# The first four blocks of a gated linear attention and MLP kernel loaded as pairs of neighbouring tokens, with a new order of the opening and w_in in fp32

## The chip, the cores and the metric

The kernel runs on one core of a Trainium2 chip. The core's engines work side by side, each through its own list of instructions in order: TensorE (PE in the profile; its weight loads are PEld), VectorE (DVE), ScalarE (ACT), GpSimd (POOL) and SyncE (SP), which here only issues transfers. Transfers run on 16 DMA engines. The metric is the time of one execution in microseconds; the median of three runs before the change is 194.14 us (193.95 to 194.42).

## The reference

Four sequences of 768 tokens with eight heads of 48 go through a gated linear attention, and its output, as rows of 384 numbers, through an MLP of width 2,048 with a squared relu.

```python
# q, k, v, alpha: (4, 8, 768, 48) fp32, alpha between 0.8 and 1
for t in range(S):
    state = alpha[:, :, t, :, None] * state + einsum('bhd,bhe->bhde', k[:, :, t], v[:, :, t])
    y[:, :, t] = einsum('bhd,bhde->bhe', q[:, :, t], state)
x = y.transpose(0, 2, 1, 3).reshape(3072, 384)
h = x @ w_in                      # 384 x 2048
r = maximum(h, 0)
out = (s * (r * r) + b) @ w_out   # 2048 x 384
```

## The kernel before

The 3,072 tokens are cut into 24 blocks of 128 tokens, six to a sequence (`NBLK`, `NCH`). A block goes through these steps; n is its number.

- Loads: alpha, k, q and v, one transfer each on SP (`load`, `load_one`, lines 121 to 127). The heads lie apart in memory, so each token and head is a run of 48 fp32 numbers, 192 B, and a block is 786 KB. Eight blocks fit at once (`NLD`).
- `ln` (ACT): logarithm of alpha. `cum` (line 191): on PE a product with an upper triangle of ones sums the logarithms along the tokens, and for the first five blocks four small products give the sum over the whole block; ACT then takes the exponential of the negative and of the positive sum. `vcast` (POOL): v in bf16.
- `qk` (DVE): k times the first exponential, q times the second. `tr`: eight PE transposes and one DVE copy to `qkT`. `amat`: eight PE products for A, then two DVE products with a triangular mask.
- `yp` (line 259): y from A and v, and from the state of the block before; also the block's part of the next state (`pst`); ACT copies y out of PSUM. `st` (POOL mainly): the new state. `xt`: three PE transposes of y and an ACT copy give the MLP's input.
- The MLP: `mp` makes 512 columns' worth of products with w_in in one PSUM bank, `rl` (ACT) the relu, `sq` (DVE) the square; `mm2` multiplies by w_out in four quarters (`o`), and ACT or DVE takes the result out. Blocks 0 and 1 form one group of 256 tokens for `mp`; each other block is a group by itself.

w_in comes in quarters of 512 columns on POOL's queue (`load_w_in`, line 129), where the transfer itself turns fp32 into bf16. w_out comes in quarters on SP and is scaled and cast on chip (`cast_w_out`). The bias and the stores of the first 14 blocks wait until later.

The order of all work is written out by hand. A list (lines 498 to 509) holds the opening: each entry is a function and its arguments, and each engine takes its instructions in the order in which the list calls them. Later blocks get positions from a formula (lines 514 to 543): block n is centred at 8n, with its steps at fixed distances; entries are sorted by position. Transfers stand in SP's list in the order of their issue: blocks 0 to 3 first (lines 440 to 446), then, from `weights_out` (line 473), w_out and blocks 4 to 7. `busy` (line 174) puts filler matmuls of 512 columns on PE whose result nobody reads; the list has sixteen of them among the first blocks. Eight PSUM banks are shared; `first_banks` says which one each piece of the opening uses.

```python
at(p - e, y, n)                                    # p = 8 * n
at(p + (2.5, 3.5, 5.5, 7.5)[u], m, group_of[n][0], u)
at(p + (8.5, 9.5, 12.5, 14.5)[u], o, n, u)
```

## Time and profile before

| | |
|---|---|
| median of three runs | 194.14 us |
| the profiled execution: its time, its span | 193.98 us, 192.2 us |
| PE, ACT, DVE, POOL busy | 94%, 61%, 77%, 34% of the span |
| chain that ended last | PE 82%, ACT 3%, DVE 2% |
| w_in products (L359) on PE, w_out products (L397) | 71.2 us busy, 68.3 us busy |
| relu (L373, ACT), one | 596 ns |
| square (L380, DVE), one | 493 ns |
| a steady block, from one w_out quarter at 76.91 to the same at 83.95 | 7.04 us |

The span runs from the first to the last instruction; the time includes what lies around it. Busy shares are averages over all stages. The chain is followed back from the last instruction to what each step waited for; 82% on PE says that for most of the span PE's own list set the pace. PE's busy time counts matmuls from start to end, and these overlap, so the distance between starts is the measure of what one costs.

### The profile page before, as it was taken

To read this page: it belongs to the slowest core of one execution; us is meant where nothing else is said; L and a number is where in the kernel's file an instruction comes from. 1 tells how busy PE (TensorE), PEld (TensorE's weight loads), DVE (VectorE), ACT (ScalarE), POOL (GpSimd) and SP (SyncE) were. 2 spreads that over 40 slices of the span, in tenths; PEclk is the share of its full clock that TensorE was granted. 3 is DMA by queue.
4 is the path that set the end of the run, shared out by engine and by line. 5 is a ranking of instruction groups with operands and counts; after the bars stand their busy time and mean duration, and the time that the engine had idled before them with its cause. 6 is when DMAs were issued, how large, how long until landed. Compare 5 with 4: busy or idle time off the path is not lost.

```text
span 192.2 us, 5966 instructions
## 1 busy us (share of the span) xinstructions
PE 179.9 (94%) x2378; PEld 143.6 (75%) x2380; DVE 148.6 (77%) x288; ACT 117.4 (61%) x240; POOL 64.4 (34%) x100
## 2 busy tenths in 40 slices
PE   0898799999999999999999999999999999999993
PEld 0575589665877788878887887887887888788782
DVE  5377877568668877988878996698988999997641
ACT  3355378815866576676676667776666657554540
POOL 6147922011310542652311562462302383262000
PEclk9999999999999999999999999999999999999999
DMA  6999999979994685682979367569958768436212
GB/s 121 190 185 185 191 223 320 326 155 192 188 153 82 132 135 91 109 151 35 206 110 162 57 114 138 107 91 195 206 118 184 148 146 164 93 121 246 85 41 82
DMA packets 113453, 28.74 MB, mean 150 GB/s; under 512 B 106627, under 2 KB 113426, under 8 KB 113426
## 3 DMA queue, kind: packets, MB, share of 16 engines
q1 hardware_dynamic: 111822, 26.79, 73.5%
q0 software_dynamic: 1600, 1.57, 5.2%
q8 instruction: 18, 0.29, 0.7%
q14 instruction: 9, 0.07, 0.1%
q10 hardware_dynamic: 4, 0.00, 0.0%
HBM read 25.19 MB, written 4.74 MB: 156 GB/s over the span
## 4 chain that ended last, share of the span: by engine, by line
PE 82%; ACT 3%; DVE 2%; issue 1%; ACTq 0%
PE h_ps L359 30%; PE o_ps L397 28%; PE ct_ps L229 5%; PE a_ps L244 3%; PE h_ps L311 2%; PE y_ps L272 2%; PE a_ps L397 2%; PE ct_ps L195 2%; PE y_ps L263 1%; PE a_ps L420 1%; PE p_ps L283 1%; ACT r_sb L373 1%; PE o_ps L359 1%; ACT w_out_bf L151 1%; PE a_ps L359 1%
## 5 line engine op out<-in xcount | busy, mean ns | idle before, releaser
L373 ACT ACTIVATE r_sb<-h_ps 128x512 bf16<-128x512 f32 x90 | 53.6, 596 | 35.0 <-PE h_ps L359 33.2
L359 PEld LDWEIGHTS <-w_in_bf 128*128 128x128 bf16 x1104 | 67.8, 98 | 6.8 <-issue 0.9
L359 PE MATMUL h_ps<-xd_all,w_in_bf 128*128 128x128 bf16 (+1 forms) x1056 | 71.2, 220 | 0.3 <-ACT xd_all L317 0.2
L397 PE MATMUL o_ps<-w_out_bf,gt_all 128*128 128x384 bf16 x336 | 68.3, 326 | 0.1
L380 DVE TENSOR_TENSOR gt_all<-r_sb 128x512 bf16<-128x512 bf16 x96 | 45.9, 493 | 25.4 <-ACT r_sb L373 24.5
L338 POOL TENSOR_TENSOR sd_sb<-t_sb,blast 48x192 bf16<-48x192 f32 x40 | 20.3, 508 | 77.7 <-DVE t_sb L333 45.2
L397 PEld LDWEIGHTS <-gt_all 128*128 128x128 bf16 x368 | 32.6, 98 | 16.2
L189 POOL CAST v_bf<-v_sb 128x384 bf16<-128x384 f32 x24 | 17.1, 717 | 32.2 <-DMA v_sb<-in_v_dram 27.6
L342 POOL TENSOR_TENSOR sc_sb<-t_sb,blast 112x384 f32<-112x384 f32 x16 | 21.6, 1347 | 1.2
L317 ACT ACTIVATE xd_all<-h_ps 128x384 bf16<-128x384 bf16 x23 | 11.3, 491 | 15.3 <-PE h_ps L311 15.3
L234 DVE COPY qkT<-ct_ps 112x1024 bf16<-112x1024 bf16 x24 | 16.4, 684 | 3.9 <-PE ct_ps L229 3.1
L252 DVE TENSOR_TENSOR am_a<-a_ps,mask 128x512 bf16<-128x512 f32 x24 | 16.4, 683 | 3.4 <-PE a_ps L244 3.4
L223 DVE TENSOR_TENSOR kb_sb<-k_sb,bi_sb 128x384 bf16<-128x384 f32 x24 | 13.7, 573 | 3.9 <-ACT bi_sb L206 3.6
L252 DVE TENSOR_TENSOR am_b<-a_ps,mask 128x512 bf16<-128x512 f32 x24 | 16.3, 680 | 0.0
L224 DVE TENSOR_TENSOR qb_sb<-q_sb,b_sb 128x384 bf16<-128x384 f32 x24 | 15.7, 655 | 0.0
L186 ACT ACTIVATE la_sb<-al_sb 128x384 bf16<-128x384 f32 x24 | 12.4, 517 | 3.8 <-DMA al_sb<-in_alpha_dram 3.7
L290 ACT ACTIVATE y_bf<-y_ps 128x384 bf16<-128x384 f32 x24 | 11.7, 490 | 4.6 <-PE y_ps L272 4.4
L229 PEld LDWEIGHTS <-qb_sb 128*112 128x112 bf16 x96 | 8.7, 136 | 5.1 <-DVE qb_sb L224 3.7
L229 PE MATMUL ct_ps<-ident,qb_sb 128*112 128x128 bf16 x96 | 10.1, 230 | 1.1 <-DVE qb_sb L224 1.1
L206 ACT ACTIVATE bi_sb<-ct_ps 128x384 f32<-128x384 f32 x20 | 9.7, 486 | 1.6 <-PE ct_ps L195 1.0
L244 PE MATMUL a_ps<-qkT 48*128 48x128 bf16 x192 | 9.8, 222 | 0.8 <-DVE qkT L234 0.4
L207 ACT ACTIVATE b_sb<-ct_ps 128x384 f32<-128x384 f32 x20 | 9.9, 494 | 0.0
(75 smaller groups left out, 196.2 us busy)
## 6 DMA issues: line engine op xcount, KB each, us to landing
al_sb<-in_alpha_dram SPq DMA_DIRECT2D x24, 192.0 KB
k_sb<-in_k_dram SPq DMA_DIRECT2D x24, 192.0 KB
q_sb<-in_q_dram SPq DMA_DIRECT2D x24, 192.0 KB
v_sb<-in_v_dram SPq DMA_DIRECT2D x24, 192.0 KB
w_out_st<-in_moe_w_out_dram SPq DMA_DIRECT2D x4, 768.0 KB
out_dram<-w_in_st SPq DMA_DIRECT2D x14, 192.0 KB
out_dram<-out_sb SPq DMA_DIRECT2D x9, 192.0 KB
w_in_bf<-in_moe_w_in_dram POOLq DMA_DIRECT2D x4, 384.0 KB, 6.6
```

What stands on the lines that cost most here:

```text
L189: nc.gpsimd.tensor_copy(out=v_bf[n % 3], in_=v_sb[n % NLD])
L224: nc.vector.tensor_tensor(out=qb_sb[n % 2][:, :, 0:48], in0=q_sb[n % NLD], in1=b_sb[n % 3], op=ALU.mult)
L229: nc.tensor.transpose(out=t_ps[0:112, x, p, :], in_=t.rearrange("a h d -> a (h d)")[:, 128 * p : 128 * p + 112], identity=ident,)
L234: nc.vector.tensor_copy(out=qkT_sb[n % 2][0:112].rearrange("a x p t -> a (x p t)"), in_=t_ps[0:112].rearrange("a x p t -> a (x p t)"),)
L244: nc.tensor.matmul(out=a_ps[e][:, p, :], lhsT=qkT[r0 : r0 + 48, 1, p, :], rhs=qkT[r0 : r0 + 48, 0, p, :], start=True, stop=True,)
L252: nc.vector.tensor_tensor(out=am_sb[e][n % 2], in0=a_ps[e], in1=mask4, op=ALU.mult)
L338: nc.gpsimd.tensor_tensor(out=sd[r, :, d], in0=t1_sb[r, :, d], in1=bl[r].to_broadcast([48, NP, 48]), op=ALU.mult)
L342: nc.gpsimd.tensor_tensor(out=sc_sb[0:112], in0=t1_sb[0:112], in1=bl[0:112].to_broadcast([112, NP, 96]), op=ALU.mult)
L359: nc.tensor.matmul(out=hp[:, jj * N : (jj + 1) * N], lhsT=w_in_bf[:, kk, 128 * j : 128 * (j + 1)], rhs=xd_sb[g][:, kk, 0:N], start=(kk == ...
L373: nc.scalar.activation(out=rs, in_=h_of.pop((g, u)), func=AF.Relu)
L380: nc.vector.tensor_tensor(out=gt_sb[g][:, u * 512 : (u + 1) * 512], in0=rs, in1=rs, op=ALU.mult)
L397: nc.tensor.matmul(out=op[:, 0:d_model], lhsT=gt_sb[g][:, j * N + t * C : j * N + (t + 1) * C], rhs=w_out_bf[:, j, :], start=(j == 0), sto ...
```

## The change

Blocks 0 and 1, and blocks 2 and 3, are loaded as pairs: 256 tokens in 128 rows, two neighbouring tokens in each row, so that a run in memory is 96 numbers, 384 B. "Block" 2i then holds the even tokens of the pair and block 2i+1 the odd ones while sums, A and the products with k and q are made; after the transposes, the copies (`qk_copy`) put q and k back so that the first 128 tokens (b = 0) and the last 128 (b = 1) can be addressed. The sums of a pair are two accumulated products each, with block-triangular matrices `D_bf` and `Ds_bf`; A is made in four parts (key parity s, head parity e) of eight small products; y and the state update take even and odd keys one after the other, with 64 rows each. The output of a pair's block is stored in two parts, of its even and its odd rows.

w_in is loaded in fp32 by SP, in the order of quarters 1, 2, 0, 3 among the other loads, and cast on ACT and DVE in twelve pieces. The group of 256 tokens goes: every block has its own `mp`. The functions of the steps are split by engine, and a new written list of 330 entries orders them as far as position 60; `rooms` gives their PSUM banks. Three filler matmuls are left. All of SP's loads up to block 7 are issued before the list. From position 60 on, the formula places the same work as before.

```diff
-    GROUPS = [2] + [1] * (NBLK - 2)
     UNITS = 5
-    assert sum(GROUPS) == NBLK
     NLD = 8
-    NFIRST = 4
+    PAIRS = [0, 2]
+    pair_of = {p + i: p for p in PAIRS for i in range(2)}
...
+    D_bf = sb.tile([128, 128], BF16, name="D_bf")
+    Ds_bf = sb.tile([128, 128], BF16, name="Ds_bf")
+    ones_p = sb.tile([128, 2], BF16, name="ones_p")
+    mask_p = [sb.tile([128, NP, 2, 64], BF16, name=f"mask_p{i}") for i in range(2)]
...
+    qkT_all = sb.tile([128, 2, 2 * NP * 128], BF16, name="qkT")
+    qkT_sb = [qkT_all[:, i].rearrange("a (x p t) -> a x p t", x=2, p=NP) for i in range(2)]
+    qkT_p = qkT_all.rearrange("a u y -> a (u y)").rearrange("a (x p b s i) -> a x p b s i", x=2, p=NP, b=2, s=2)
...
+    def load_pair(n, name):
+        whole, t = {"al": (al_all, alpha), "k": (k_all, k), "q": (q_all, q), "v": (v_all, v)}[name]
+        b, c = n // NCH, n % NCH
+        nc.sync.dma_start(
+            out=whole[:, n % NLD : n % NLD + 2].rearrange("a u x -> a (u x)").rearrange("a (h x) -> a h x", h=H),
+            in_=t[b, :, c * C : (c + 2) * C, :].rearrange("h (r s) d -> r h (s d)", s=2),
+        )
...
     def load_w_in(i):
         cols = slice(i * d_ff // 4, (i + 1) * d_ff // 4)
-        nc.gpsimd.dma_start(
-            out=w_in_bf[:, :, cols], in_=moe_w_in[:, cols].rearrange("(t r) f -> r t f", t=KT)
-        )
+        nc.sync.dma_start(out=w_in_st[:, :, cols], in_=moe_w_in[:, cols].rearrange("(t r) f -> r t f", t=KT))
+
+    def cast_w_in(i, kk, act):
+        cols = slice(i * d_ff // 4, (i + 1) * d_ff // 4)
+        if act:
+            nc.scalar.activation(out=w_in_bf[:, kk, cols], in_=w_in_st[:, kk, cols], func=AF.Copy)
+        else:
+            nc.vector.tensor_copy(out=w_in_bf[:, kk, cols], in_=w_in_st[:, kk, cols])
...
-    def busy(n, bank=o_ps):
+    def busy(n, key):
         for i in range(n):
             nc.tensor.matmul(
-                out=bank,
-                lhsT=U_bf,
-                rhs=mask4.rearrange("a p t -> a (p t)"),
+                out=room(key),
+                lhsT=D_bf,
+                rhs=mask_p[0].rearrange("a p s t -> a (p s t)"),
...
+    def cum_pair(n):
+        for s, m in ((0, D_bf), (1, D_bf if n > pair_of[n] else Ds_bf)):
+            nc.tensor.matmul(
+                out=room(("c", n))[:, 0:384], lhsT=m, rhs=la_sb[s][:, :, 0:48], start=(s == 0), stop=(s == 1)
+            )
+
+    def tot_pair(n):
+        for p in range(NP):
+            for s in range(2):
+                nc.tensor.matmul(
+                    out=room(("t", n))[0:112, 400 + 2 * p : 402 + 2 * p],
+                    lhsT=la_sb[s].rearrange("a h d -> a (h d)")[:, 128 * p : 128 * p + 112],
+                    rhs=ones_p,
+                    start=(s == 0),
+                    stop=(s == 1),
+                )
+
...
+    def qk_copy(n):
+        if n in pair_of:
+            nc.vector.tensor_copy(
+                out=qkT_p[0:112, :, :, :, n - pair_of[n]].rearrange("a x p b i -> a (x p) b i"),
+                in_=t_ps[0:112].rearrange("a x p (b i) -> a (x p) b i", b=2),
+            )
+            return
...
+    def amat_pair(n, s, e):
+
+        bank = room(("A", n, s, e)).rearrange("a (p x) -> a p x", p=NP)
+        r = slice(64 * e, 64 * e + 48)
+        for p in range(NP):
+            for b in range(2):
+                cols = slice(64 * b, 64 * b + 64)
+                nc.tensor.matmul(
+                    out=bank[cols, p, :],
+                    lhsT=qkT_p[r, 1, p, b, s],
+                    rhs=qkT_p[r, 0, p, b].rearrange("a s i -> a (s i)"),
+                    start=True,
+                    stop=True,
+                )
+
+    def mask_pair(n, s, e):
+        nc.vector.tensor_tensor(
+            out=am_sb[e][s].rearrange("a p t -> a (p t)"),
+            in0=room(("A", n, s, e)),
+            in1=mask_p[s].rearrange("a p s t -> a (p s t)"),
+            op=ALU.mult,
+        )
+
+    def y_pair(n):
+        p0 = pair_of[n]
+        c = n % NCH
+        rows = slice(64 * (n - p0), 64 * (n - p0) + 64)
+        if c > 0:
+            for p in range(NP):
+                nc.tensor.matmul(
+                    out=y_ps[:, 96 * p : 96 * p + 96],
+                    lhsT=qkT_p[0:112, 0, p, n - p0].rearrange("a s i -> a (s i)"),
+                    rhs=sd_sb[(n - 1) % 2][0:112, p, :],
+                    start=(p == 0),
+                    stop=False,
+                    skip_group_check=True,
+                )
+        for h in range(H):
+            for s in range(2):
+                nc.tensor.matmul(
+                    out=y_ps[:, 48 * h : 48 * h + 48],
+                    lhsT=am_sb[h % 2][s][rows, h // 2, :],
+                    rhs=v_bf[(p0 + s) % 3][rows, h, :],
+                    start=(c == 0 and h == 0 and s == 0),
+                    stop=(h == H - 1 and s == 1),
+                    skip_group_check=True,
+                )
+
+    def pst_pair(n):
+        p0 = pair_of[n]
+        rows = slice(64 * (n - p0), 64 * (n - p0) + 64)
+        for p in range(NP):
+            for s in range(2):
+                nc.tensor.matmul(
+                    out=pst[:, p, :],
+                    lhsT=kb_sb[(p0 + s) % 3].rearrange("a h d -> a (h d)")[rows, 128 * p : 128 * p + 128],
+                    rhs=v_bf[(p0 + s) % 3][rows, 2 * p : 2 * p + 2, :],
+                    start=(s == 0),
+                    stop=(s == 1),
+                )
+
...
+    rooms = {
+        ("A", 0, 0, 0): a1, ("A", 0, 0, 1): h1, ("A", 0, 1, 0): a0, ("A", 0, 1, 1): a1, ("A", 2, 0, 0): ct,
+        ("A", 2, 0, 1): o, ("A", 2, 1, 0): a1, ("A", 2, 1, 1): h1, ("c", 0): ct, ("c", 1): a0, ("c", 2): h0,
...
+    def mp(n, u):
+        hp = room((n, u))
+        for jj in range(4):
+            j = 4 * u + jj
             for kk in range(KT):
                 nc.tensor.matmul(
-                    out=hp[:, jj * N : (jj + 1) * N],
+                    out=hp[:, jj * C : (jj + 1) * C],
                     lhsT=w_in_bf[:, kk, 128 * j : 128 * (j + 1)],
-                    rhs=xd_sb[g][:, kk, 0:N],
+                    rhs=xd_sb[n][:, kk],
...
     def store(n, o):
+        if n in pair_of:
+            rows = out[n * C : (n + 1) * C, :].rearrange("(i s) m -> s i m", s=2)
+            for s in range(2):
+                nc.sync.dma_start(out=rows[s], in_=o[64 * s : 64 * s + 64])
+            return
...
+    load_pair(0, "al")
+    load_pair(0, "k")
+    load_pair(0, "q")
+    load_pair(0, "v")
+    load_pair(2, "al")
+    load_pair(2, "q")
+    load_pair(2, "v")
+    load_pair(2, "k")
+    load_one(4, al_sb, alpha)
+    load_w_in(1)
+    load_w_in(2)
+    load_w_in(0)
+    load_one(4, k_sb, k)
+    load_one(4, q_sb, q)
+    load_one(4, v_sb, v)
+    load_one(5, al_sb, alpha)
+    load_w_in(3)
+    load_one(5, q_sb, q)
+    load_one(5, k_sb, k)
+    load_one(6, al_sb, alpha)
+    load_one(5, v_sb, v)
+    load_one(6, q_sb, q)
+    load_one(6, k_sb, k)
+    load_w_out(0, 4)
+    load_w_out(4, 8)
+    load_one(6, v_sb, v)
+    load_w_out(8, 12)
+    load_w_out(12, 16)
+    load_one(7, al_sb, alpha)
+    load_one(7, q_sb, q)
+    load_one(7, v_sb, v)
+    load_one(7, k_sb, k)
...
-            (ln, 0), (vcast, 0), (cum, 0), (qk, 0), (spread,), (busy, 2), (tr, 0), (ln, 1), (busy, 1), (vcast, 1), (amat, 0), (cum, 1),
-            (busy, 3), (yp, 0), (qk, 1), (st, 0), (busy, 1), (tr, 1), (ln, 2), (xt, 0), (vcast, 2), (load_w_in, 0), (load_w_in, 1), (cum, 2), (busy, 1), (amat, 1),
-            (busy, 3), (yp, 1), (qk, 2), (st, 1), (busy, 1), (tr, 2), (ln, 3), (xt, 1), (load_w_in, 2), (vcast, 3), (load_w_in, 3), (cum, 3), (busy, 1), (amat, 2),
...
+            (spread,), (ln, 0), (ln, 1), (busy, 1, ("c", 0)), (cum_pair, 0), (cum_act, 0), (cum_pair, 1), (cum_act, 1),
+            (pst_pe, 5), (kb_mul, 0), (qb_mul, 0), (vcast, 0), (qb_mul, 1), (tot_pair, 0), (busy, 1, ("T", 0)),
+            (tr, 0, 0), (tr, 0, 1), (kb_mul, 1), (qk_copy, 0), (vcast, 1), (busy, 1, ("T", 1)), (tr, 1, 0), (tr, 1, 1),
+            (qk_copy, 1), (pst_pair, 0), (tot_act, 0), (ln, 3), (ln, 2), (cum_pair, 2), (amat_pair, 0, 1, 1), (t1, 0),
+            (cum_act, 2), (amat_pair, 0, 0, 1), (mask_pair, 0, 1, 1), (sd, 0), (vcast, 2), (amat_pair, 0, 0, 0),
+            (qb_mul, 2), (mask_pair, 0, 0, 1), (amat_pair, 0, 1, 0), (cum_pair, 3), (tot_pair, 2), (tr, 2, 0),
+            (mask_pair, 0, 0, 0), (cum_act, 3), (mask_pair, 0, 1, 0), (y_pair, 0), (kb_mul, 2), (pst_pair, 1),
+            (qb_mul, 3), (y_act, 0), (tr, 2, 1), (y_pair, 1), (xt_pe, 0), (tot_act, 2), (ln, 4), (kb_mul, 3),
+            (qk_copy, 2), (vcast, 3), (y_act, 1), (cast_w_in, 1, 1, True), (xt_act, 0), (tr, 3, 0), (t1, 1), (tr, 3, 1),
+            (cum_pe, 4), (pst_pair, 2), (sd, 1), (xt_pe, 1), (qk_copy, 3), (amat_pair, 2, 0, 0), (xt_act, 1),
+            (cum_act, 4), (cast_w_in, 2, 2, True), (cast_w_in, 2, 0, True), (cast_w_in, 2, 1, True),
+            (cast_w_in, 1, 2, False), (cast_w_in, 1, 0, False), (amat_pair, 2, 1, 0), (mask_pair, 2, 0, 0), (t1, 2),
+            (mp, 0, 1), (rl, 0, 1), (amat_pair, 2, 0, 1), (amat_pair, 2, 1, 1), (pst_pair, 3), (mp, 1, 1), (sd, 2),
+            (mask_pair, 2, 1, 0), (mask_pair, 2, 0, 1), (mask_pair, 2, 1, 1), (rl, 1, 1), (mp, 1, 2),
+            (cast_w_in, 0, 1, False), (cast_w_in, 0, 2, False), (cast_w_in, 0, 0, True), (y_pair, 2), (mp, 0, 2),
+            (mp, 0, 0), (rl, 1, 2), (y_act, 2), (rl, 0, 2), (sq, 0, 1), (qb_mul, 4), (xt_pe, 2), (y_pair, 3), (tr, 4, 0),
+            (kb_mul, 4), (t1, 3), (sq, 0, 2), (rl, 0, 0), (vcast, 4), (tr, 4, 1), (mp, 1, 0), (xt_act, 2), (y_act, 3),
+            (ln, 5), (rl, 1, 0), (sd, 3), (xt_pe, 3), (pst_pe, 4), (mp, 2, 1), (qk_copy, 4), (xt_act, 3), (rl, 2, 1),
+            (amat, 4), (cum_pe, 5), (cum_act, 5), (mp, 3, 2), (sq, 1, 1), (sq, 1, 2), (mask, 4, 1), (mask, 4, 0),
+            (mp, 3, 0), (sq, 0, 0), (cast_w_in, 3, 1, False), (cast_w_in, 3, 2, False), (qb_mul, 5), (rl, 3, 2),
+            (cast_w_in, 3, 0, True), (t1, 5), (mp, 2, 2), (mp, 2, 0), (y_pe, 4), (rl, 3, 0), (mp, 1, 3), (rl, 2, 2),
+            (y_act, 4), (rl, 1, 3), (tr, 5, 0), (xt_pe, 4), (rl, 2, 0), (xt_act, 4), (ln, 6), (kb_mul, 5), (sq, 3, 2),
+            (tr, 5, 1), (t1, 4), (sq, 3, 0), (sq, 2, 2), (qk_copy, 5), (mp, 0, 3), (sq, 1, 0), (rl, 0, 3), (mp, 2, 3),
+            (mp, 4, 0), (cum_pe, 6), (sq, 2, 1), (amat, 5), (rl, 2, 3), (mp, 4, 2), (cum_act, 6), (mask, 5, 0),
+            (mp, 4, 1), (mask, 5, 1), (vcast, 5), (sd, 4), (rl, 4, 2), (rl, 4, 0), (sq, 2, 0), (kb_mul, 6), (mp, 4, 3),
+            (qb_mul, 6), (sq, 4, 0), (sq, 1, 3), (rl, 4, 1), (y_pe, 5), (rl, 4, 3), (cast_w_out, 0, 2, False),
+            (vcast, 6), (y_act, 5), (mp, 3, 1), (mp, 3, 3), (vcast, 7), (load, 8), (cast_w_out, 2, 4, True), (tr, 6, 0),
+            (tr, 6, 1), (xt_pe, 5), (o_pe, 0, 0), (o_pe, 1, 0), (xt_act, 5), (o_pe, 4, 0), (sd, 5), (rl, 3, 3),
...
+    def late(pos, *what):
+        for fn, *args in what:
+            if pos >= OPEN:
+                at(pos, fn, *args)
```

## The prediction

> **What bounds the kernel now.** I read the page's slices first, then the TensorE timeline, then the landings of the loads in the ACT and POOL timelines.
>
> ```profile
> span 192.2 us, 5966 instructions
> PE   0898799999999999999999999999999999999993
> PEclk9999999999999999999999999999999999999999
> DMA  6999999979994685682979367569958768436212
> GB/s 121 190 185 185 191 223 320 326 155 192 188 153 82 132 135 91 109 151 35 206 110 162 57 114 138 107 91 195 206 118 184 148 146 164 93 121 246 85 41 82
> DMA packets 113453, 28.74 MB, mean 150 GB/s; under 512 B 106627, under 2 KB 113426, under 8 KB 113426
> ```
>
> A slice is 4.8 us. PE is full from slice 5 on, so it bounds the kernel. In the first five slices the DMA engines are full and move only 185 to 191 GB/s: these are the loads of blocks 0 to 3, rows of 192 B. In slices 6 and 7 (w_out, rows of 1,536 B) the same engines move 320.
>
> ```profile
> 4.51 0.48 PE L195 MATMUL h_ps<-la_sb,U_bf 128*128 128x384 bf16 x1 [4.51 <-ACT la_sb L186]
> ...
> 9.98 1.44 PE L176 MATMUL o_ps<-mask,U_bf 128*128 128x512 bf16 x3
> ...
> 14.95 0.82 PE L176 MATMUL o_ps<-mask,U_bf 128*128 128x512 bf16 x3
> ...
> 22.44 0.82 PE L359 MATMUL h_ps<-xd_all,w_in_bf 128*128 128x256 bf16 x6
> ...
> 71.69 0.81 PE L397 MATMUL o_ps<-w_out_bf,gt_all 128*128 128x384 bf16 x4
> ```
>
> Columns: start, time taken, operation. The three filler matmuls (L176) take 1.44 us at 9.98 and 0.82 us at 14.95: up to about 14.6 us PE runs at half speed, though the slices show PEclk as 9. The first product with w_in (L359) starts at 22.44. At 71.69 stands the third of the four w_out products of block 6. Both kernels issue the same work from there on, in one order, so 192.2 - 71.7 = 120.5 us are common, and the change lives in front of this point, which I call the cut.
>
> ```profile
> 3.93 0.52 ACT L186 ACTIVATE la_sb<-al_sb 128x384 bf16<-128x384 f32 x1 [1.92 <-DMA al_sb<-in_alpha_dram]
> ```
>
> ```profile
> 7.05 0.50 POOL L189 CAST v_bf<-v_sb 128x384 bf16<-128x384 f32 x1 [3.17 <-DMA v_sb<-in_v_dram]
> 11.26 0.84 POOL L189 CAST v_bf<-v_sb 128x384 bf16<-128x384 f32 x1 [3.71 <-DMA v_sb<-in_v_dram]
> ...
> 15.44 0.50 POOL L189 CAST v_bf<-v_sb 128x384 bf16<-128x384 f32 x1 [0.64 <-DMA v_sb<-in_v_dram]
> 15.89 1.70 POOL L131 DMA_DIRECT2D w_in_bf<-in_moe_w_in_dram  x2
> ```
>
> v of blocks 0, 1, 2 lands every 4.2 us: 786 KB a block, 187 GB/s. The first two quarters of w_in are issued from 15.89; the trace gives these transfers 6.3 to 7.4 us to landing, so w_in is there at 22.2 and the product at 22.44 starts with it.
>
> **How tight PE is after 22.44.** Start-to-start costs at full clock, from the steady stage: four PSUM-quarter products with w_in (12 matmuls) 0.67, four with w_out 0.65, eight transposes 0.45, the eight A matmuls 0.33, cumulative sum 0.165, y 0.20 plus 0.17 with a state, state update and x transposes 0.165 each. Before the cut, from 22.44: 8x0.655 + 22x0.67 + 26x0.65 for the products, 2.25 transposes (5), 1.98 A (6), 1.16 sums, 1.68 y, 0.66 state, 0.83 x: 45.4 us of work in 49.25. A steady block takes 7.04 us against 6.93 by the same prices (1.6%), so 45.4 becomes 46.1 and 3.1 us are stalls.
>
> **The change, part by part.**
> *Pair loads.* Eight loads of 384-B rows replace sixteen of 192 B. No 384-B row is in the trace. Its single packets take 15 ns at 192 B, 35 at 768 B, 65 at 1,536 B (medians); on the line 384 B takes 22. Streaming, 192 B costs 16.4 ns per engine (187 GB/s), 9% more than its packet; so 384 B costs 23.3, 264 GB/s and 1.49 us a pair load. Bounds: 187 GB/s (bytes decide, 2.1 us) and 374 (packets decide, 1.05 us). I take 1.49, the middle row's value.
> [...]
>
> *Landings.* First packet at 1.9, a load is usable 1.15 after its last packet (0.93 for the first). alpha 0/1 then 4.4 (3.93 before, but for two blocks), k 6.05, q 7.5, v 8.95, alpha 2/3 10.4, q 11.9, v 13.3, k 14.8, alpha 4 15.8. The w_in quarters now go in fp32 on SP, behind nine loads instead of sixteen; their bytes read are the old ones (3.1 MB, some 375 GB/s read), 2.1 us a quarter: 17.9, 20.0, 22.1, the fourth 28.4 behind block 4. ACT's queue holds a cast of the first quarter ahead of x of block 0 and reaches it at 18.9, 1.0 after the landing; were the quarter later than that, x of 0 and 1 and the exponentials of 4 would wait behind it. w_out stands behind blocks 4 to 6: first quarter 36.8, last 44.2 (before, its first cast ran at 31.84).
>
> *Up to the first product.* ln of both blocks 4.4 to 5.3; sums and exponentials to 7.5 (0.39 a step on ACT); q at 7.5 sets qb, two DVE products to 8.55, transposes in the half clock 0.86, copy 0.69, a filler, transposes of block 1 and its copy: 12.1. State update and the sums of 2/3 meanwhile to 12.5. Four A calls, eight matmuls each: bounds 0.33 and 0.45 at full clock, twice that before (rows L244, and transposes of the same width); two write one bank with a mask (0.69) between. Masks end 16.4. Then y, update, transposes of 2 and 3, two copies, y of 1, x of 0 and 1, on a chain PE, ACT, DVE to the last copy at 20.3 to 20.8; two w_in casts on DVE (0.4 each, from 1.02 for 1536 columns) beside two A calls: first product at 21.5, if full clock comes by 18. Gain 0.9 against 22.44. Even and odd tokens double the matmuls of A, sums, y and update in blocks 0 to 3; most of that lies ahead of 21.5 under these waits.
>
> *After the first product.* 30x0.67 + 26x0.65 = 37.0; transposes 2.25, A 1.65, sums 0.83, y 1.31, update 0.50, x 0.99; left of the pairs: y of 2 and 3 (sixteen matmuls at 25 ns + 0.17, twice) 1.14, two A calls 0.9, an update 0.33. Sum 46.9, with 1.6% 47.65.
>
> *Stalls.* I walked the three queues with these durations through the first 20 products. No bank, relu or quarter is late by more than 0.1 us: w_in's fourth quarter is needed at 32.7 (lands 28.4), w_out's first at 40.8 (36.8). The load on ACT and DVE is near PE's: in these 19.7 us ACT has 20 relus at 0.49, eight y and x copies, two logarithms and four exponentials at 0.39 and five casts at 0.5, 17.8 us; DVE some 16. So I keep 1.0 of the old 3.1 us.
>
> *The rest costs nothing.* Twenty-two mask and triangle instructions on POOL instead of twelve (0.29 for 128 columns; the four 512-wide ones, by that row, up to 0.8) end near 8.2, under v at 8.95; bare they would shift block 0's update only. Twelve casts: 3.0 us ACT, 2.4 DVE, inside the stall term. Four more stores of unchanged 1,536-B rows go out late, at a DMA share of 0.4 to 0.7; uncovered, one issue of 0.5 us each.
>
> *Sum.* 21.5 + 47.65 + 1.0 = 70.15 at the cut, 1.54 before 71.69. The profiled execution took 193.98, its span 192.2; 193.98 - 1.54 = 192.44, and as the median of the runs, 194.14, lies 0.16 higher, 192.6.
>
> **Rivals.**
> *The clock opens late.* Sixteen fillers become three, and PE waits more before 11 us. Before, half speed lasted until 14.6 although PE was busy 4.48 of 5 us from 5 to 10. From 12.5 on the new order is dense in half clock, which speaks for an opening at 15 to 18. At 21.4, y, transposes and sums of 13 us double: first product near 23, time 194.1. An opening at 24.8 halves the next 1.8 us too, 0.9 more: 195.0. It turns slower from an opening at about 24 us.
> [...]
>
> *Pairs buy nothing (187 GB/s).* k of 2/3 lands at 19.9 instead of 14.8; kb of block 2, 4.9 us ahead of the first product, then starts it at 24.8: 3.3 later, time 195.9, slower. It decides where k eats its slack of 1.45 and the gain of 1.54: eight loads at 1.86 us, under 211 GB/s. Against it: a 768-B packet takes 2.3 times as long as one of 192 B for four times the bytes.
>
> *The order stalls as before.* In-order ACT holds casts of w_in ahead of relus; with 3.1 us of stalls the cut is 72.25: 194.7; with 2.5, 194.1.
>
> *Better than thought.* 374 GB/s and an open clock by 15: first product 20.2, stalls 0.4: 190.7.
>
> **Chances.** Forecast (191.4 to 193.7) 0.52; clock 0.15; pairs 0.10; stalls 0.14; better 0.09. A change is told from none at 0.2%, 0.4 us. Faster: forecast, better and a little of the stall case, 0.63; within: half of the stall case and an early form of the clock case, 0.13; slower 0.24. The range reaches from the best case to a late clock or nearly the slow pairs: 190.7 to 195.4; the forecast's own is 191.4 to 193.7.
>
> **What would show it.** The profile after should have ln of blocks 0 and 1 at 4.4, v cast near 9, first w_in product at 21 to 22, full-speed matmuls by 18, first w_out product near 41, and block 6's third w_out quarter at 70. GB/s of slices 1 and 2 near 260 confirms the pairs; 190 refutes them. PE idle beyond 0.3 us after 22 with ACT or DVE as releaser would show the order wrong; matmuls of 0.43 for four transposes beyond 20 us, the clock.

## The result, and the profile after

The changed kernel is slower: 197.33 us median (196.76 to 197.38, 4 runs) against 194.08 for the kernel before beside it, ratio 1.0158 (95% interval 1.0135 to 1.0181). The forecast was 192.6 and the range ended at 195.4. Here and below, a ratio leaves out runs that are more than 1.5% above the fastest of the same kernel. The profiled execution took 197.38 us with a span of 195.6.

The page of the kernel after: span, slices of 4.9 us, and the chain that ended last.

```profile
span 195.6 us, 6229 instructions
PE   1899999999999999999999999999999999999993
PEclk9999999999999999999999999999999999999999
GB/s 165 322 319 370 146 266 176 359 346 124 91 199 40 161 120 96 112 83 203 45 158 73 101 158 87 85 196 179 41 191 114 223 106 172 126 124 121 82 42 80
PE 94%; DVE 3%; issue 0%; ACT 0%; DVEq 0%; ACTq 0%
```

What the change was written to do, it does. In the second slice, which holds nothing but loads of pairs, 322 GB/s are moved (185 to 191 before; the 370 of the fourth slice is mostly w_in), and PE is full from the third slice on. PE's share of the chain rose from 82% to 94%: hardly anything but PE sets the pace any more. Yet the kernel is slower, so PE has more to do or works more slowly somewhere. The row of clocks shows nothing of it. The timeline of PE in the kernel after does (start, time taken, operation):

```profile
16.37 0.65 PE L289 MATMUL ct_ps<-ident,qb_sb 128*112 128x128 bf16 x4
...
23.94 1.46 PE L491 MATMUL h_ps<-xd_all,w_in_bf 128*128 128x128 bf16 x12
...
30.82 2.04 PE L491 MATMUL h_ps<-xd_all,w_in_bf 128*128 128x128 bf16 x24
...
34.12 0.83 PE L491 MATMUL a_ps<-xd_all,w_in_bf 128*128 128x128 bf16 x12
...
47.68 1.46 PE L522 MATMUL h_ps<-w_out_bf,gt_all 128*128 128x384 bf16 x8
...
73.95 2.11 PE L522 MATMUL o_ps<-w_out_bf,gt_all 128*128 128x384 bf16 x12
```

The first product with w_in takes 1.46 us at 23.94, the same twelve matmuls take 0.83 at 34.12, and the row at 30.82 is half one and half the other. PE ran at half speed up to about 32 us, where it had left half speed at 14.6 before. The cut (the third quarter of the row at 73.95, each 0.65) stands at 75.25 instead of 71.69: 3.56 later, and the two spans differ by 3.4. Of the 3.56, 1.50 arose before the first product (23.94 against 22.44) and 2.06 behind it (51.31 against 49.25).

The trace also holds the throttle's own record: when full clock was granted, from the first instruction on. Its first entries are those at 14.53 and 31.96: it has none for the half-speed start, which is why the slices show 9 from the start.

```
kernel   full clock granted (from, to)
before   14.53 to 192.02 (the span ends at 192.18)
after    31.96 to the end (195.57)
```

### The profile page after: what moved, and what is told of

Same layout as the page of the kernel before. It is cut to its first block, busy times and chain, and to the rows that moved or that the text cites. A ratio compares the mean times of both kernels' runs of the same rounds, so it can differ in the third digit from the quotient of the medians.

```text
span 195.6 us, 6229 instructions
## 1 busy us (share of the span) xinstructions
PE 186.8 (96%) x2499; PEld 152.4 (78%) x2499; DVE 148.7 (76%) x299; ACT 120.0 (61%) x249; POOL 66.8 (34%) x106
## 2 busy tenths in 40 slices
DMA packets 105198, 30.33 MB, mean 155 GB/s; under 512 B 98371, under 2 KB 103634, under 8 KB 105170
## 4 chain that ended last, share of the span: by engine, by line
PE 94%; DVE 3%; issue 0%; ACT 0%; DVEq 0%; ACTq 0%
PE h_ps L491 27%; PE o_ps L522 26%; PE ct_ps L289 7%; PE h_ps L522 5%; PE a_ps L491 3%; PE a_ps L312 3%; PE ct_ps L491 2%; PE y_ps L397 2%; PE ct_ps L224 2%; PE o_ps L491 2%; PE p_ps L376 1%; PE h_ps L447 1%; PE p_ps L410 1%; PE y_ps L388 1%; PE y_ps L362 1%; PE a_ps L548 1%
## 5 line engine op out<-in xcount | busy, mean ns | idle before, releaser
L491 PEld LDWEIGHTS <-w_in_bf 128*128 128x128 bf16 x1152 | 70.6, 100 | 5.7 <-issue 0.3
L504 ACT ACTIVATE r_sb<-h_ps 128x512 bf16<-128x512 f32 x77 | 45.8, 596 | 30.8 <-PE h_ps L491 29.1
L491 PE MATMUL h_ps<-xd_all,w_in_bf 128*128 128x128 bf16 x924 | 62.5, 221 | 0.0
L522 PE MATMUL o_ps<-w_out_bf,gt_all 128*128 128x384 bf16 x304 | 61.3, 326 | 0.1
L284 DVE TENSOR_TENSOR qb_sb<-q_sb,b_sb 128x384 bf16<-128x384 f32 x24 | 16.4, 681 | 2.0 <-ACT b_sb L238 2.0
L302 DVE COPY qkT<-ct_ps 112x1024 bf16<-112x1024 bf16 x20 | 13.6, 682 | 3.9 <-PE ct_ps L289 3.3
L321 DVE TENSOR_TENSOR am_a<-a_ps,mask 128x512 bf16<-128x512 f32 x20 | 13.6, 681 | 1.1 <-PE a_ps L312 1.1
L454 ACT ACTIVATE xd_all<-h_ps 128x384 bf16<-128x384 bf16 x16 | 7.8, 490 | 10.4 <-PE h_ps L447 10.4
L321 DVE TENSOR_TENSOR am_b<-a_ps,mask 128x512 bf16<-128x512 f32 x20 | 13.6, 680 | 0.7 <-PE a_ps L312 0.7
L522 PE MATMUL h_ps<-w_out_bf,gt_all 128*128 128x384 bf16 x64 | 11.9, 326 | 0.0
L289 PE MATMUL ct_ps<-ident,kb_sb 128*112 128x128 bf16 x96 | 10.3, 235 | 0.0
```

Source lines behind the costliest of these rows:

```text
L284: nc.vector.tensor_tensor(out=qb_sb[n % 2][:, :, 0:48], in0=raw("q", n), in1=b_sb[n % 3], op=ALU.mult)
L289: nc.tensor.transpose(out=t_ps[0:112, x, p, :], in_=t.rearrange("a h d -> a (h d)")[:, 128 * p : 128 * p + 112], identity=ident,)
L302: nc.vector.tensor_copy(out=qkT_sb[n % 2][0:112].rearrange("a x p t -> a (x p t)"), in_=t_ps[0:112].rearrange("a x p t -> a (x p t)"),)
L321: nc.vector.tensor_tensor(out=am_sb[e][n % 2], in0=a_ps[e], in1=mask4, op=ALU.mult)
L491: nc.tensor.matmul(out=hp[:, jj * C : (jj + 1) * C], lhsT=w_in_bf[:, kk, 128 * j : 128 * (j + 1)], rhs=xd_sb[n][:, kk], start=(kk == 0), s ...
L504: nc.scalar.activation(out=rs, in_=room((g, u)), func=AF.Relu)
```

## The experiments

All times are us; "first" is the start of the first product with w_in and "cut" the point named in the prediction, both of the profiled execution. The medians of the kernel before, measured beside them, are 193.88 to 194.21. The fillers write PSUM banks that are overwritten later and are read by nothing.

| kernel | runs, median (lowest to highest) | ratio to before, 95% | full clock in the profiled run | first | cut |
|---|---|---|---|---|---|
| after | 197.33 (196.76 to 197.38) | 1.0135 to 1.0181 | from 31.96 | 23.94 | 75.25 |
| e1_early | 196.23 (189.58 to 196.99) | - | 5.66 to 9.07, from 29.55 | 23.67 | 74.13 |
| e4_early_small | 197.0 (196.77 to 197.32) | 1.0125 to 1.018 | from 31.86 | 23.95 | 75.21 |
| e2_spread | 190.27 (189.87 to 190.47) | 0.9783 to 0.9831 | from 10.24 | 19.98 | 68.23 |
| e14_spread_small | 198.34 (197.85 to 198.85) | 1.0137 to 1.0235 | from 32.10 | 25.37 | 76.13 |
| e8_gap_only | listed below | - | from 10.30 | 19.69 | - |
| e7_both | listed below | - | from 5.63 | 18.95 | - |
| e6_win_pool | listed below | - | 9.85 to 16.68, from 30.33 | 22.10 | - |
| e5_runs192 | 198.06 (197.83 to 199.23) | 1.0148 to 1.0267 | 8.68 to 18.92, from 32.58 | 24.16 | - |
| e3_before_few | 195.95 (195.52 to 196.79) | 1.0074 to 1.0141 | from 27.49 | 23.34 | 74.55 |
| e9_hold | 190.75 (190.32 to 191.01) | 0.9775 to 0.9861 | from 9.78 | 20.60 | 68.63 |
| e10_all | 190.06 (189.64 to 190.55) | 0.9742 to 0.9828 | from 6.22 | 19.85 | 67.88 |
| e11_runs192_hold | 195.29 (193.69 to 198.54) | 0.9976 to 1.0065 | from 8.53 | 23.36 | 71.37 |
| e12_win_pool_hold | 190.49 (189.99 to 191.33) | 0.9768 to 0.9855 | from 8.22 | 20.04 | 68.09 |
| e13_before_early | 195.02 (194.6 to 196.0) | 1.0 to 1.0065 | from 5.15 | 22.21 | 73.00 |

The theory drawn from this: the change cut the fillers from sixteen to three and gave the pairs' matmuls only 48 or 64 of the array's rows, so the clock stays at half until the products with w_in come; everything else works as predicted. The rivals: the new order itself stalls or the pairs' additional matmuls cost more than expected, the loads are no faster in effect, or the fp32 w_in and its casts cost time.

### Fillers put back, and fillers taken from the kernel before

e2_spread adds seven fillers of 128x512 to the kernel after, at three places, two of them waits of PE; e3_before_few takes thirteen of the sixteen out of the kernel before.

```diff
 # e2_spread
+    def busy_y(n):
+        for i in range(n):
+            nc.tensor.matmul(out=y_ps, lhsT=D_bf, rhs=mask_p[0].rearrange("a p s t -> a (p s t)"), ...)
-   (tot_pair, 0), (busy, 1, ("T", 0)),
+   (tot_pair, 0), (busy_y, 2), (busy, 1, ("T", 0)),
-   (vcast, 1), (busy, 1, ("T", 1)),
+   (vcast, 1), (busy_y, 3), (busy, 1, ("T", 1)),
-   (vcast, 2), (amat_pair, 0, 0, 0),
+   (vcast, 2), (busy_y, 2), (amat_pair, 0, 0, 0),
```

> The changed kernel with seven more filler matmuls of 512 columns between 7 and 14 us (2 after the sums, 3 in the wait before the second transposes, 2 in the wait before the third A call), so that ten stand ahead of 14 us as about eight did before. Clock theory: full clock by 15 to 18 us, time 191.5 to 194. Rival (pair matmuls with 48 or 64 rows hold the clock down whatever stands between them): full clock still after 25 us, time 197 to 198.5, since seven fillers cost up to 3 us at half speed.

> The kernel before with three filler matmuls instead of sixteen, nothing else changed. Clock theory: full clock only some 4 to 9 us after the first dense products at 22.4, so at 26 to 32 us, and time 196 to 199. Rival (fillers are not what opened the clock): full clock near 14.5 as before, time 193.5 to 194.3.

PE's timeline in e2_spread:

```profile
9.30 1.28 PE L221 MATMUL y_ps<-mask_p,D_bf 128*128 128x512 bf16 x3
...
10.63 0.39 PE L299 MATMUL ct_ps<-ident,qb_sb 128*112 128x128 bf16 x4
...
19.98 0.84 PE L501 MATMUL h_ps<-xd_all,w_in_bf 128*128 128x128 bf16 x12
...
40.66 1.46 PE L532 MATMUL h_ps<-w_out_bf,gt_all 128*128 128x384 bf16 x8
...
66.93 2.11 PE L532 MATMUL o_ps<-w_out_bf,gt_all 128*128 128x384 bf16 x12
```

With seven more matmuls whose results nobody reads, the kernel is 7.06 us faster than the changed one and 1.9% faster than the kernel before. Transposes take 0.39 already at 10.63 (0.65 at 16.37 in the kernel after). The cut is 7.02 earlier: 3.96 of it before the first product, 3.06 behind it. Clock and time are both better than expected (15 to 18 us, 191.5 to 194). So the clock took the whole loss, and the gain that would have been there, provided that it isn't the mere filling of PE's time that helps; e14_spread_small, below, tests that.

The kernel before loses only 2.1 us (1.1%; 195.95 against 193.88 beside it) when its clock opens at 27.49 instead of 14.53; 196 to 199 had been expected. PE's timeline in e3_before_few:

```profile
22.12 0.67 PE L229 MATMUL ct_ps<-ident,qb_sb 128*112 128x128 bf16 x4 [0.46 <-DVE qb_sb L224]
...
23.34 1.49 PE L359 MATMUL h_ps<-xd_all,w_in_bf 128*128 128x256 bf16 x6
...
74.55 0.81 PE L397 MATMUL o_ps<-w_out_bf,gt_all 128*128 128x384 bf16 x4
```

There PE still waits in the opening even at half speed (0.46 in brackets, for a product that DVE makes), and the time of the thirteen fillers themselves is gone, so the first product comes only 0.90 later (23.34 against 22.44). In the kernel after, PE is busy without a gap from 15 us on, and its first product comes 3.96 later than e2_spread's, although that kernel has seven fillers more to do.

### What in a filler opens the clock

e1_early puts 24 fillers of 128 rows by 128 columns into PE's idle time before the first logarithm; e4_early_small the same number and time with 48 rows and 64 columns.

```diff
 # e1_early
+    def early(n):
+        for i in range(n):
+            nc.tensor.matmul(out=y_ps[:, 0:128], lhsT=D_bf, rhs=D_bf, start=True, stop=True)
-            (spread,), (ln, 0),
+            (early, 24), (spread,), (ln, 0),
 # e4_early_small, in place of the matmul above
+            nc.tensor.matmul(out=y_ps[0:64, 0:128], lhsT=D_bf[0:48, 0:64], rhs=D_bf[0:48], ...)
 # e14_spread_small: e2_spread, with busy_y's matmul cut to
+            out=y_ps[0:64], lhsT=D_bf[0:48, 0:64], rhs=mask_p[0]...[0:48]
```

> The changed kernel with 24 filler matmuls (128x128 weights, 128 columns) into the idle y bank ahead of everything else on PE, in the time (about 1.6 to 4.3 us) in which PE waits anyway. Clock theory (the changed order keeps PE busy but not with enough matmul work, so the full clock comes at 32 us instead of 14.5, and that alone is the loss): full clock by about 15 us, first w_in product at 21 to 22 us, time 191 to 193.5. Rival A (what counts is work just before the opening, not at the start): full clock stays at 28 to 32 us, time 196.5 to 197.5. Rival B (the loss is the extra matmuls of the pairs, the casts or the order): even with an early clock the time stays above 195.

> As the first of these four, with fillers of 48 rows and 64 columns of weights (128 moving columns), the shape of the pairs' A matmuls: the same count in the same place. If the clock follows the time in which PE is busy, it is like the first kernel, full clock by about 15 us and 191 to 193.5. If it follows how much of the array works, full clock stays near 32 us and the time at 196.5 to 197.5.

e1_early opened the clock at 5.66 and lost it at 9.07. Of its ten runs one took 189.58 and the others 194.0 to 197.0; in eight of these nine the mean granted clock is 0.945 to 0.965: early work alone didn't hold it there. The median, 196.23, fits neither the 191 to 193.5 of the clock theory nor the 196.5 to 197.5 of rival A, and the run at 189.58 speaks against rival B. In the profiled execution of e4_early_small the clock opened at 31.86, and all four runs stayed at the changed kernel's time. Because e1's times scatter, the two don't part cleanly; the shape was tried again where the clock opens in every run:

> e2_spread with the same seven fillers at the same places, but of 48 rows by 64 columns of the array in place of 128 by 128; each still moves 512 columns, so that TensorE is busy for as long. Theory (the gate counts how much of the array works): the clock opens as late as in the changed kernel, 27 to 32 us, and the time is 196.5 to 198 in nearly every run. Rival (the gate counts how long TensorE is busy, and e2 is faster because its waits are filled): open at 10 to 11 us and 190.0 to 190.8 as e2.

The stretches of e14_spread_small (length, then busy time and instructions of PE, PEld, DVE, ACT, POOL; PEclk, DMA share, GB/s), and below it one line of its timeline of PE:

```profile
5.00:10.00 5.00, 5.00 (x25) 2.86 (x24) 2.54 (x6) 2.86 (x9) 4.29 (x13) 1.00 1.17 323
10.00:15.00 5.00, 5.00 (x40) 2.94 (x39) 1.99 (x4) 1.04 (x3) 0.88 (x2) 1.00 1.12 312
15.00:20.00 5.00, 5.00 (x62) 3.83 (x59) 4.51 (x8) 1.63 (x6) 1.72 (x3) 1.00 1.06 367
20.00:25.00 5.00, 5.00 (x62) 4.34 (x62) 2.73 (x6) 2.18 (x6) 3.13 (x4) 1.00 0.82 166
```

```profile
25.37 1.46 PE L505 MATMUL h_ps<-xd_all,w_in_bf 128*128 128x128 bf16 x12
```

PE was busy for every one of these twenty microseconds, and at 25.37 it was still at half speed; the clock opened at 32.10 and the time is 198.34, 8 us above e2_spread. The only difference in the code is the share of the array that seven fillers use. The rival (busy time opens the clock) falls here.

### How few fillers are enough, and what closes the clock again

e8_gap_only keeps only the three fillers of e2_spread ahead of block 1's transposes; e7_both has e1's and e2's fillers; e6_win_pool is e2_spread with w_in converted in its transfer on GpSimd's queue again, without casts. In the recorded texts the gate is what grants the full clock, and a window is a step of its record: e1_early's clock was open for one of 3.41 us. PE had been busy for 3.41 of the 3.41 us before it opened at 5.66, and for 1.98 of the 3.41 us before it closed at 9.07.

> The changed kernel with only the three fillers that fall into the wait before block 1's transposes (8.9 to 9.7 us). If these suffice for one window: full clock by 14 us, 190 to 191.5. If the window needs more (the kernel before had some eight ahead of 14.5): full clock late in some or all executions, times spread from 190 to 197.

> The changed kernel with the seven fillers of the second experiment and the 24 early ones of the first together. If the gate opens after one window with enough work and closes after a window with too little, the early ones open it at 5 to 9 us and the later ones keep it open: 189 to 190, every run below 191. If early opening is worth nothing because loads and DVE set the pace before 12 us: 190.2 to 190.6.

> The changed kernel with the seven fillers, but w_in again converted in the transfer on the POOL queue (issued behind v of block 1, quarters in the order 1, 2, 0, 3), and none of the twelve casts. If w_in in fp32 on SP is a part of the gain: four issues of 0.8 us on POOL hold back block 0's state and the transfers share the engines with the loads, first product at 21.5 or later, 191.5 to 194. If it is worth nothing or costs (twelve casts gone from ACT and DVE): 189.5 to 190.6.

All three scatter. For e8 that was expected if three fillers are too few; for e7, with every run expected below 191, and for e6 it was not. The runs: e8 190.05, 195.06, 195.83, 196.29; e7 189.45, 189.58, 190.77, 195.27; e6 189.68, 190.08, 194.93, 195.65. In the runs from 194.9 to 196.3 the mean granted clock is 0.962 to 0.972, in the others 0.998 to 1.0: there the clock opened and closed again. The profiled execution of e6_win_pool is one of them, open from 9.85, closed at 16.68, open again from 30.33. PE's groups in its stretch from 13.27 to 16.68 (busy and mean ns, then idle time ahead of them):

```profile
L372 PE MATMUL y_ps<-v_bf,am_a 64*128 64x48 bf16 x8 | 0.7, 183 | 0.6 <-DVE am_a L349 0.6
L340 PE MATMUL a_ps<-qkT 48*64 48x128 bf16 x16 | 0.6, 217 | 0.1
L265 PE MATMUL h_ps<-ones_p,la_sb 128*112 128x2 bf16 x8 | 0.5, 187 | 0.0
```

PE waits 0.6 us of the 3.41 there, and much of the rest are matmuls of 48 or 64 rows or of two columns: the pairs' own work. So six fillers were put among it:

```diff
 # e9_hold: e2_spread, and (e10_all: e7_both, e12_win_pool_hold: e6_win_pool with the same lines)
-   (mask_pair, 0, 1, 0), (y_pair, 0), (kb_mul, 2), (pst_pair, 1),
+   (mask_pair, 0, 1, 0), (busy_y, 1), (y_pair, 0), (kb_mul, 2), (pst_pair, 1), (busy, 2, ("A", 2, 1, 0)),
-   (qk_copy, 2), (vcast, 3),
+   (qk_copy, 2), (busy, 2, ("A", 2, 1, 0)), (vcast, 3),
-   (pst_pair, 2), (sd, 1),
+   (pst_pair, 2), (busy, 1, ("A", 2, 1, 0)), (sd, 1),
```

> e2_spread (the changed kernel with 7 fillers of 128x512 more, 190.27 us) and in addition six more of them inside the pairs' masked sums and state updates, where TensorE's own matmuls use 48 or 64 rows: one ahead of the first pair's y, two after the first state update of block 1, two after the second pair's copies are asked for, one after the state update of block 2. At full clock six of them are 1.3 us of TensorE time, part of it in waits that stand there now (0.4 us at 15.6). Theory (the gate closes again when a stretch of 3.4 us holds too little matmul work, and that is what spread e5, e6, e7 and e8 over 189.5 to 198 us): every run between 189.9 and 191.3, clock open at 10 to 11 us and never closed before the end. Rival (the gate follows the phase of its grid alone, and more work in the pair section does nothing): a spread as in e6 and e7, with runs of 194 to 196 among them. Rival (e2 needs no hold, the fillers only cost): all runs 0.8 to 1.3 us above e2, 191.1 to 191.6.

> e7_both (24 small fillers from 1.5 us on, and the seven of e2) with the six hold fillers of e9. Theory: the clock opens at about 5.6 us and cannot close, so that no run is at 195 as one of e7 was; 189.3 to 190.3, which is 0.4 to 0.8 us under e9, since the work between 5.6 and 10.2 us runs at full speed, if that work and not the landings sets the first masked sums. Rival (the early landings set them: the same as e9 within 0.2 us). Rival (the early fillers open the gate too soon, it closes before the first copies as in e1 and opens late): runs of 194 to 197 among them.

> e6_win_pool (w_in converted in its transfer on GpSimd's queue as before the change, with no cast on the engines; everything else as in e2) with the six hold fillers of e9. Theory (the fp32 load of w_in with casts is worth nothing beside e2: the first product is held by TensorE's own pair work): within 0.5 us of e9. Rival (the casts cost DVE and ACT time that the masks and squares wait for): 1 us or more under e9. Rival (the transfer on GpSimd's queue lands later than the fp32 one and GpSimd's issues hold up the masks or the casts of v): 1 us or more over e9. If single runs lie at 194 to 196 the clock closed in them, and the rest are compared.

With these fillers no run lies above 191.4 in any of the three: e9_hold 190.32 to 191.01, e10_all 189.64 to 190.55, e12_win_pool_hold 189.99 to 191.33. The hold fillers cost 0.2 to 0.5 us against e2_spread (ratios 0.9818 and 0.9807, medians 190.75 and 190.27), whose four runs held without them. Small fillers weren't tried in their place. e10_all is the fastest that is also steady: 190.06, ratio 0.9785. Its gain over e9 is 0.69, in the predicted 0.4 to 0.8. e12 is 0.26 under e9, within the 0.5 that was given for no difference: the fp32 load of w_in and its twelve casts are worth about nothing beside the rest.

### What the 384-byte runs are worth

e5_runs192 cuts each pair load of e2_spread into two transfers of 192-byte runs with the same layout in SBUF; e11_runs192_hold adds the six hold fillers and six more in its longer waits.

```diff
-        nc.sync.dma_start(out=whole[...], in_=t[...].rearrange("h (r s) d -> r h (s d)", s=2))
+        for s in range(2):
+            nc.sync.dma_start(out=slot(whole, n + s), in_=t[...].rearrange("h (r s) d -> s r h d", s=2)[s])
```

> The changed kernel with the seven fillers (time 190.3), but each pair load cut into two transfers of 192-B runs that put the same data in the same places. If the 384-B runs are what brings the first product forward: sixteen transfers at about 190 GB/s end near 18.4 us instead of about 11.5, k of blocks 2 and 3 is usable at 19.5, the first w_in product starts at 24 to 25, and the time is 193.5 to 196, no better than the kernel before. If the loads are hidden behind the opening's chain: first product near 20, 190 to 191.

> e5_runs192 (each pair load cut into two transfers of 192-byte runs, everything else as in e2) with the six hold fillers of e9 and six more in the two waits that e5 has for late loads (four ahead of the second pair's sums, two more before block 3's copies). It is meant to show what the 384-byte runs are worth with the clock open, which e5 could not. Theory (the pair loads move 1.6 to 1.8 times the bytes in a microsecond, and all eight are done some 4 to 6 us earlier): with the clock open from 10 us on, the first product with w_in comes at 22 to 24 us in place of 20, and the time is 192.5 to 194.5. Rival (the loads are ahead of TensorE anyway, so the runs' length is worth nothing): 190.3 to 191.3, as e9. Rival (the clock closes again in the longer waits, as in e5): 196 to 198, and then the question stays open.

e5 measured 198.06 but settles nothing: its clock, open at 8.68, was closed from 18.92 to 32.58. In e11 the clock stayed open in the profiled execution. The logarithms of blocks 2 and 3 in ACT's timeline, and the first product in PE's, of e11_runs192_hold:

```profile
12.13 0.94 ACT L227 ACTIVATE la_sb<-al_sb 128x384 bf16<-128x384 f32 x2 [4.28 <-DMA al_sb<-in_alpha_dram]
```

```profile
23.36 0.84 PE L502 MATMUL h_ps<-xd_all,w_in_bf 128*128 128x128 bf16 x12 [0.65 <-DVE w_in_bf L164]
```

Two lines of DVE's timeline in the same run show what DVE had waited for up to that cast: k of block 3, and then w_in, which stands behind the pair loads in SP's queue.

```profile
18.98 0.56 DVE L292 TENSOR_TENSOR kb_sb<-k_sb,bi_sb 128x384 bf16<-128x384 f32 x1 [1.04 <-DMA k_sb<-in_k_dram]
...
21.91 1.39 DVE L164 CAST w_in_bf<-w_in_st 128x512 bf16<-128x512 f32 x2 [0.29 <-DMA w_in_st<-in_moe_w_in_dram]
```

ACT's and PE's lines of e9_hold, which differs in the loads and in six fillers, are:

```profile
9.33 0.94 ACT L226 ACTIVATE la_sb<-al_sb 128x384 bf16<-128x384 f32 x2 [1.49 <-DMA al_sb<-in_alpha_dram]
```

```profile
20.60 0.84 PE L501 MATMUL h_ps<-xd_all,w_in_bf 128*128 128x128 bf16 x12
```

The second pair's alpha is used 2.80 us later, the first product waits for a w_in cast and starts 2.76 later, and the cut is 2.74 later (71.37 against 68.63). The runs scatter from 193.69 to 198.54 with a median 4.5 above e9; the lowest five, 193.69 to 194.14, are about 3 above it. That the extra above this is the clock in every such run isn't shown: three of the four highest have a mean clock of 0.982 to 0.991, the rest 1.0 or close to it, and a late opening would leave the mean at 1.0 too (it is 1.0 in the kernel after, which opens at 31.96). Without the wide runs the new order is no better than the kernel before (ratio 1.002, over nine of the twelve runs).

### Is it only an earlier clock?

e2 opens 4.3 us earlier than the kernel before. e13_before_early opens the clock of the kernel before early, and leaves its loads and blocks.

```diff
-  (ln, 0), (vcast, 0), ... (tr, 0), (ln, 1), (busy, 1),
+  (early, 24), (ln, 0), (vcast, 0), ... (tr, 0), (ln, 1), (busy, 2),
```

> The kernel before with 24 small fillers (128 rows, 128 columns) from the point where the triangle is built, and one more of its own fillers in the wait ahead of the first A; its loads, its blocks and its sixteen fillers stay. It is to say how much of the 3.8 us that e2 lies under the kernel before is the clock (open at 10.24 against 14.53) and how much the pairs. Theory (the pairs are worth it: before's loads of 192-byte runs set its opening, and its first product with w_in at 22.44 waits for a landing, not for TensorE): 193.0 to 194.3 with the clock open at 6 to 10 us. Rival (what e2 gains is the earlier clock alone): 189.8 to 191.5. Rival (the early fillers make the clock close again before block 1, as in e1): runs of 195 to 198 among them.

PE's timeline of e13_before_early, with the idle time ahead of an operation and its releaser in brackets:

```profile
12.89 0.32 PE L199 MATMUL h_ps<-la_sb,U_bf 128*128 128x384 bf16 x1 [1.05 <-ACT la_sb L190]
...
16.55 0.43 PE L233 MATMUL ct_ps<-ident,qb_sb 128*112 128x128 bf16 x4 [0.72 <-DVE qb_sb L228]
...
18.19 0.32 PE L199 MATMUL h_ps<-la_sb,U_bf 128*128 128x384 bf16 x1 [0.82 <-ACT la_sb L190]
...
22.21 0.82 PE L363 MATMUL h_ps<-xd_all,w_in_bf 128*128 128x256 bf16 x6
```

Two of the waits are for ACT's logarithms, and ACT waits for the landing of alpha:

```profile
12.32 0.52 ACT L190 ACTIVATE la_sb<-al_sb 128x384 bf16<-128x384 f32 x1 [1.35 <-DMA al_sb<-in_alpha_dram]
...
17.62 0.52 ACT L190 ACTIVATE la_sb<-al_sb 128x384 bf16<-128x384 f32 x1 [1.43 <-DMA al_sb<-in_alpha_dram]
```

Full clock from 5.15 on gains 0.23 us at the first product; the rest turns into waits, for the next block's loads above all. The median is even 0.9 above the kernel before, more than the 193.0 to 194.3 expected, though the ratio's interval (1.0 to 1.0065) reaches down to no change: w_out's first cast starts at 33.52 instead of 31.84, after a fourth w_in transfer that was issued at 22.93 instead of 21.27. Why that order slipped wasn't tried. So the 3.6 us by which e2_spread beats the kernel before (190.27 against 193.88 beside it) are not the earlier clock alone. They need both: loads that are fast enough to keep PE in work, and a clock that lets it work.

## Why the prediction was wrong

**The step that failed** stands in "Up to the first product": "first product at 21.5, if full clock comes by 18", with the fillers' removal priced only in the rival. That rival had the mechanism and the sign, but 0.15 of the chance and too early a bound: "An opening at 24.8 halves the next 1.8 us too ... 195.0." The argument was "From 12.5 on the new order is dense in half clock, which speaks for an opening at 15 to 18." It is dense in time: PE was busy 5.00 of 5 us in both of these stretches of the kernel after,

```profile
15.00:20.00 5.00, 5.00 (x66) 4.22 (x65) 4.07 (x9) 1.92 (x7) 0.41 (x2) 1.00 1.05 358
20.00:25.00 5.00, 5.00 (x54) 4.37 (x54) 3.12 (x7) 3.31 (x9) 3.17 (x5) 1.00 0.73 142
```

and the clock still opened only at 31.96. e14 against e2 shows what counted instead (32.10 against 10.24). The argument goes by busy time; e14's rows, 5.00 of 5 us busy and closed, don't agree with it. The openings at 18, 21.4 and 24.8 are the author's assumptions, which no run shows; the runs showed 31.96, and 10.24 with the fillers of e2.

**What the step cost.** The first product came at 23.94 instead of 21.5 (2.44 more), and from there to the cut took 51.31 instead of 48.65 (2.66 more). Together 5.10; 192.44 + 5.10 is 197.54, against 197.38 measured for that execution. The 21.5 itself stays untested: it was meant for an opening by 18, and no profiled execution of the new order opened between 10.30 and 29.55 us.

**Pair loads: right mechanism, size off.** Taken: 1.49 us a load, 264 GB/s, from the line between packet times. SP, whose queue the loads fill, issues one every 1.19 us:

```profile
5.44 1.15 SPq L149 DMA_DIRECT2D q_sb<-in_q_dram  x1
6.63 1.15 SPq L149 DMA_DIRECT2D v_sb<-in_v_dram  x1
7.82 1.15 SPq L149 DMA_DIRECT2D k_sb<-in_k_dram  x1
```

393 KB in 1.19 us is 330 GB/s, nearer to the bound where packets decide (374) than to the middle. A 384-byte packet took 22 ns (median over the trace of the kernel after), just as the line gave. The term that was mis-sized is the step from a packet to the stream: the prediction added 9% (22 and 9% would be 24.0, where it has 23.3), but 1,024 runs in 1.19 us on 16 engines are 18.6 ns a run, 15% less than the packet. The 9% came from 15 ns, the 192-byte median over the whole run; up to 18 us, while the loads stream, that median is 20, more than the 16.4 of the stream, so packets overlap there. The bound of 187 is refuted by the second slice (322), and the 2.1 us a load that goes with it falls too. Logarithms of 0 and 1 were forecast at 4.4 and came at 4.32; those of 2 and 3 started at 9.15, where alpha was expected at 10.4. v's cast, forecast at 9, came at 8.44, as soon as POOL's mask instructions were done, so it doesn't show the landing of v.

**Pairs buy nothing** was refuted as a rival, but its price was good: it gave 195.9 and a first product 3.3 us later; e11 measured 2.76 later and 3 us or more, with a wait for k on the way, as that rival had it.

**After the first product: right, given the clock.** 46.9 of work, 47.65 with its allowance and 1.0 of stalls were predicted; e2_spread, at full clock from 10.24, takes 48.25 from 19.98 to the cut. Its first product with w_out at 40.66 stands where 40.8 was forecast. So "the order stalls as before" falls too, and the casts cost nothing that shows (e12). The "better" rival, with its first product at 20.2 and 190.7, is what e2 and e9 became: 190.27 and 190.75. It named the open clock as a condition; nothing in the change supplied it.

## What to carry to other kernels

Before matmuls that look idle are taken out, ask whether they hold the clock, and count array work and not busy time: transposes and matmuls, mainly of 48 or 64 rows, kept PE busy for 5.00 of 5 us here from 15 to 20 without opening it before 31.96. A late clock cost less while PE waited for loads and other engines anyway (2.1 us for an opening 13.0 us later in the kernel before) than once it didn't (7.1 us for one 21.7 later here, twice as much for each microsecond), so removing a transfer bound and removing the fillers that its waits hid are one change, to be priced together. When a result scatters between two times, read the granted clock of each run before explaining the median; and because the start at half speed isn't in that record here (it begins at 14.53 and 31.96), look at the durations of equal matmuls too.

## What the runs showed of the hardware that had not been expected

- **The clock changed on a grid.** The record of e1_early is open for 3.41 us, closed for 20.48, open for 163.84; e6's has 6.83 and 13.65, e5's 10.24 and 13.65. All are multiples of 3.413 (1, 6, 48, 2, 4, 3, 4), as is the 177.49 for which it was open in the kernel before (52).
- **Fillers that use more of the array opened the clock earlier.** e2 and e14 issue the same fillers at the same places, of 128x128 and 48x64 of the array: 10.24 against 32.10. Whether rows, columns or their product counts wasn't tried, nor whether the values in the fillers matter.
- **It closed again with PE busy for most of the time.** In e6 PE was busy 2.78 of the 3.41 us before it closed at 16.68, with light matmuls; e13 stayed open with 3.15 of 5 us busy between 15 and 20. So fewer idle microseconds aren't what held it in these two.
- **Runs of 384 bytes moved 322 to 330 GB/s** on SP's queue (by the second slice, and by 393 KB in 1.19 us), against 185 to 191 for 192 bytes. The slices of the kernel before that the prediction calls 6 and 7, mainly runs of 1,536 bytes, moved 320 and 326, and the fourth slice of the kernel after, mainly runs of 2,048 bytes, 370, where the prediction had put some 375 for w_in.
